# The first two raw chunks of a weight, loaded early into an idle input buffer

## The chip, the core and the metric

The kernel runs on one core of a Trainium2 chip. The core has a matrix engine (PE in the rows, with its weight loads as PEld), VectorE (DVE), ScalarE (ACT), GpSimd (POOL) and SyncE (SP, SPq for its queue of DMA issues); sixteen DMA engines move data between HBM and the on-chip memory (SBUF). The metric is device microseconds (us) of one execution, the median of the timed runs; lower is better.

## What is computed

Masked attention over 2 batches of 8 heads (768 tokens, head size 64), then two feed-forward layers on the 1536 tokens it gives (512 columns, 2048 inner columns). Cut to what matters:

```python
scores = scale * np.matmul(q, k.transpose(0, 1, 3, 2))
scores = np.where(mask, scores, -1000000000.0)     # mask: the 6-bit buckets of q and k agree
attn = softmax(scores)
x = np.matmul(attn, v)                             # per head, then (1536, 512)

h = x @ w_in                                       # first layer
g = np.where(h > 0.0, h, np.exp(np.minimum(h, 0.0)) - 1.0)
x = g @ w_out

h = x @ w_in2                                      # second layer
r = np.maximum(h, 0.0)
out = (s * (r * r) + b) @ w_out2
```

The weights arrive as 8-byte floats.

## The kernel before

**Attention** goes in units: unit u is one head of one chunk of 128 queries, 96 units in all; units 0 to 47 are batch 0 (chunks 0 to 5), 48 to 95 batch 1. A unit has its scores on PE (L358), the row maximum on DVE (L368), the exponential on ACT (L370), and then a split of the result into a high and a low 16-bit half: ACT copies the high half (L389), GpSimd subtracts (L392, tile `ph`), and SP issues a transposing DMA (L394, tile `pt`). PE then multiplies `pt` with the values (L412, tile `xacc`). The first 16 units take another way, through PE transposes (L379, L406). Three `ph` buffers rotate. After the eighth head of a chunk the result is normalised and laid into one of three input buffers `xx[0..2]` of the first layer, 512 tokens each; `xx[1]` (x_114 in an instruction's operands) is for tokens 512 to 1023, so nothing is written to it before chunk 4. `xx[2]` (x_115) serves, while it is idle, as a place for raw keys, queries and values of batch 1.

**Weights of the first layer** are streamed by the generator `w_stream`, one chunk of 512 KB per step: a step splits chunk n-3 into halves, decodes chunk n-2, and issues the load of chunk n into one of three `wraw` buffers (L167). Decoding is three DVE instructions (L194, L195, L197: an 8-byte float becomes a 4-byte one). Splitting is a copy on ACT (L188, tiles `wih`, `woh`) and a subtraction: on DVE (L204), or, for chunks that count as set aside, on GpSimd, which then also scales the chunk (L187, then L202):

```python
aside_ = n_ - 3 < aside
if aside_:
    nc.gpsimd.tensor_scalar(w, w, SW, None, op0=ALU.mult)
```

Here n_ is the step. The 16 chunks of `w_in` have 12 set aside, the 16 chunks of `w_out` none. The stream of `w_in` starts at unit 2, that of `w_out` is chained behind it once the first layer's products run.

**The first layer** (`moe1`) goes over six blocks of 256 tokens: `up` multiplies with `w_in` (L531, tile `h`), `down` with `w_out` (L531, tile `x2p`). Its products and the steps of attention are woven together by a credit count; two of three product slots also take a step of the weight stream (`w1_step`). When 40 units have been started and the stream isn't through, the rest of it is run through at once, ahead of any further unit:

```python
while live["w1"] and nxt["s"] >= (C - 1) * H:
    w1_step()
```

In what follows this stretch is called the drain. The second layer (`up2`, `down2`) runs after that, with attention over. A scheduler with a modelled clock puts the instructions of each engine in order, so that a new instruction also shifts its neighbours.

Of the kernel before, what the change touches and what calls it, by code (L numbers as in the profile page):

```python
# [10 lines left out]
I32 = mybir.dt.int32  # L11
# [50 lines left out]
SC_N = 16  # L62
PRE = 4
W_FROM = 2
LN2 = 0.6931471805599453


def model_kernel(tc, q, k, v, proj, w_in, w_out, w_in2, w_out2, s2, b2, sel, pop, eye, out):
    nc = tc.nc
# [23 lines left out]
    with ExitStack() as base:  # L93
# [50 lines left out]
        def w_raw(st):  # L144
            return pool(st, "wraw", WRAW, side="right")


        def w_tiles(p, nm):
            return [p.tile([128, KF, 512], F16, name=f"{nm}{x}") for x in "hl"]

        def w_in_chunks(dst, dram):
            w = dram.bitcast(I32)
            return [((lambda a, f=f: dst(f)) if callable(dst) else [d[:, f, :] for d in dst], w[:, 256 * f:256 * f + 256].rearrange("(k p) n -> p k n", p=128))
                    for f in range(KF)]

        def w_col_chunks(dst, dram):
            w = dram.bitcast(I32)
            return [([z[:, f:f + 4, 128 * d:128 * d + 128] for z in dst],
                     w[128 * f:128 * f + 512, 256 * d:256 * d + 256].rearrange("(k p) n -> p k n", p=128))
                    for d in range(KM) for f in range(0, KF, 4)]  # L160

        def w_load(ch, wraw):
            t = wraw.tile([128, 512, 2], I32, tag="w", name="wraw")
            o = t.rearrange("p n t -> p (n t)")
            if len(ch[1].shape) == 3:
                o = o.rearrange("p (k n) -> p k n", k=ch[1].shape[1])
            nc.sync.dma_start(out=o, in_=ch[1])  # L167
            return t

        def w_stream(chunks, wraw, words, delay=0, aside=0):  # L170
            loaded, joined = [], []
            for n_, ch in enumerate(chunks + [None] * 3):
                with late_by(delay):
                    done = joined.pop(0) if joined else None
                    if done:
                        (dst, _), w = done
                        w = w.bitcast(F32)
                        if callable(dst):
                            dst = dst(w)
                            done = dst and (None, w)  # L180
                    if done:
                        hi, lo = dst
                        if len(hi.shape) == 3:
                            w = w.rearrange("p (k n) -> p k n", k=hi.shape[1])
# [3 lines that stand above are left out]
                        nc.scalar.activation(out=hi, in_=w, func=ACTF.Copy, scale=1.0 if aside_ else SW)  # L188
                    if len(loaded) == 2 or (ch is None and loaded):
                        c0, t = loaded.pop(0)  # L190
                        a, x = words()
                        a, x = a.bitcast(I32), x.bitcast(I32)
                        low, top = t[:, :, 0], t[:, :, 1]
                        nc.vector.tensor_scalar(x, top, 3, 0x3FFFFFFF, op0=ALU.logical_shift_left, op1=ALU.bitwise_and)  # L194
                        nc.vector.scalar_tensor_tensor(out=x, in0=low, scalar=29, in1=x,  # L195
                                                       op0=ALU.logical_shift_right, op1=ALU.bitwise_or)
                        nc.vector.scalar_tensor_tensor(out=a, in0=top, scalar=-0x40000000, in1=x,  # L197
                                                       op0=ALU.bitwise_and, op1=ALU.bitwise_or)
                        joined.append((c0, a))
                    if done:  # L200
                        if aside_:
                            nc.gpsimd.tensor_tensor(out=lo, in0=w, in1=hi, op=ALU.subtract)  # L202
                        else:
                            nc.vector.scalar_tensor_tensor(out=lo, in0=w, scalar=SW, in1=hi,  # L204
                                                           op0=ALU.mult, op1=ALU.subtract)
                    if ch is not None:
                        loaded.append((ch, w_load(ch, wraw)))
                yield
# [153 lines left out]
        def u_soft(u):  # L362
# [5 lines left out]
            nc.vector.tensor_scalar(f, sps.pop(u), CLAMP, None, op0=ALU.min, op1=ALU.min, accum_out=mx)  # L368
            (nc.gpsimd if U0 <= u < MXP else nc.vector).tensor_scalar(mx, mx, sm / (SQ * SQ), 10.0 * LN2, op0=ALU.mult, op1=ALU.add)  # L369
            nc.scalar.activation(out=f, in_=f, func=ACTF.Exp, scale=-sm / (SQ * SQ), bias=mx,  # L370
# [44 lines left out]
        xx = [xs_.tile([128, 2 * KM, 512], F16, name=f"x{i}") for i in range(B * C // 4)]  # L415
# [53 lines left out]
        nxt = {"s": 0, "av": 0, "soft": [], "split": [], "lag": LAG0}  # L469
# [339 lines left out]
        if True:  # L809
# [3 lines left out]
            for hp, nm in ((0, "k"), (0, "q"), (1, "k"), (1, "q")):  # L813
# [5 lines left out]
            wdec = w_raw(wdst), lambda: (wst.tile([128, 512], F32, tag="wa", name="wa"),  # L819
                                         ring.take("w", [128, 512], F32, "wx"))  # L820
            ws1 = w_stream(w_in_chunks(wi, w_in), *wdec, aside=ASIDE)
            n = 0
            for _ in att:
                n += 1
                if nxt["s"] >= W_FROM and n % WN == 0:
                    next(ws1, None)
                if done_chunks[0] == BLOCKS1[0]:
                    break
# [12 lines left out]
                gp[0] = pool(gst1, "gp1", 1)  # L841

            wo = w_tiles(wop, "wo")
            ws1 = chain(ws1, w_stream(w_col_chunks(wo, w_out), *wdec))
            live = {"w1": True, "att": True}
            credit = 0.0

# [24 lines left out]
            for ks, cost in enumerate(moe1(wi, wo, gp, next_gp, tmp, tmpg, att_step)):  # L872
# [7 lines left out]
                if not live["att"] and ws2 is None:  # L880
# [5 lines left out]
                    wraw = w_raw(wlate)  # L886
# [12 lines left out]
                    ch = ci[:W2PRE]  # L899
# [80 lines left out]
```

## Time and profile before

| what | value |
|---|---|
| runs, median (lowest to highest) | 716.36 us (713.94 to 717.16) |
| profiled execution, its own time | 715.27 us |
| its span | 713.5 us |
| PE busy | 659.6 us, 92% |
| DVE busy | 516.6 us, 72% |
| ACT busy | 417.2 us, 58% |
| GpSimd busy | 272.7 us, 38% |
| mean granted clock of PE | 0.986 |

The own time is what the runs measure; the span is the stretch that the trace covers, 1.8 us less. Busy shares are means over stages that are unlike each other.

### The profile page before, as it was taken

Reading aid. Unit: us, or ns where it says so; the run is one execution under the profiler, and the core shown is the slowest. Engines: PE = TensorE matmul, PEld = TensorE weight load, DVE = VectorE, ACT = ScalarE, POOL = GpSimd, SP = SyncE. Lnnn points to the kernel's source line nnn. Section 1 sums busy time; section 2 is a strip of 40 time slices with the busy share of each in tenths; the row PEclk is TensorE's granted clock in tenths of the full one; section 3 lists DMA queues with packets and bytes.
Section 4 is the critical chain, followed back from the end, with each engine's and each line's share of the span. In section 5 each row is a group of like instructions: output and inputs, shape, how many; then the busy total and the mean of one; then the engine's idle time right before and its main releaser. Section 6 shows DMA issues by size and latency. Waiting matters only on the chain.

```text
span 713.5 us, 15214 instructions
## 1 busy us (share of the span) xinstructions
PE 659.6 (92%) x6192; PEld 504.0 (71%) x6192; DVE 516.6 (72%) x885; ACT 417.2 (58%) x687; POOL 272.7 (38%) x219
## 2 busy tenths in 40 slices
PE   2789869888887999999999999999999999999998
PEld 0368657676666777888888988874444446888887
DVE  5688899888878468645744699439999726999730
ACT  2897679874797887756755333234555525555520
POOL 1257778873445278945854421311211200000000
PEclk9999979999999999999999999999999999999999
DMA  9984599999899588966768545004453000000100
GB/s 234 259 222 135 159 223 225 205 229 219 178 208 215 88 142 159 154 119 123 123 112 120 132 153 175 1 25 125 121 149 115 0 1 1 16 30 32 45 30 30
DMA packets 206742, 89.73 MB, mean 126 GB/s; under 512 B 171856, under 2 KB 203344, under 8 KB 206672
## 3 DMA queue, kind: packets, MB, share of 16 engines
q1 hardware_dynamic: 206080, 88.63, 56.4%
q8 instruction: 48, 0.79, 0.5%
q10 hardware_dynamic: 592, 0.14, 0.1%
q14 instruction: 22, 0.18, 0.1%
HBM read 43.13 MB, written 3.15 MB: 65 GB/s over the span
## 4 chain that ended last, share of the span: by engine, by line
PE 59%; DMA 11%; ACT 10%; DVE 7%; issue 6%; POOL 5%; SPq 0%; DVEq 0%; ACTq 0%; POOLq 0%
PE h L531 24%; PE y L775 15%; PE x2p L531 10%; DMA pt<-ph 6%; PE s L358 4%; POOL ph L392 3%; ACT p L370 3%; PE xacc L412 3%; ACT ph L389 2%; PE xacc L406 1%; DVE e L546 1%; DMA k<-src 1%; ACT gh L551 1%; PE pT L379 1%; DVE p L368 1%
## 5 line engine op out<-in xcount | busy, mean ns | idle before, releaser
L392 POOL TENSOR_TENSOR ph<-p,ph 128x768 f16<-128x768 f32 x80 | 133.9, 1679 | 65.3 <-ACT ph L389 45.7
L531 PE MATMUL h<-x,wih 128*128 128x256 f16 x768 | 132.5, 276 | 0.1
L531 PE MATMUL h<-x,wi 128*128 128x512 f16 x576 | 124.5, 379 | 0.0
L368 DVE TENSOR_SCALAR_CACHE_REDUCE p<-s 128x768 f32<-128x768 f32 x96 | 91.0, 950 | 44.4 <-PE s L358 42.1
L370 ACT ACTIVATE p<-p,mx 128x768 f32<-128x768 f32 x96 | 89.1, 928 | 46.4 <-DVE mx L369 40.5
L775 PE MATMUL y<-wqh,a 128*128 128x256 f16 x672 | 110.3, 273 | 0.0
L775 PEld LDWEIGHTS <-a 128*128 128x128 f16 x1008 | 98.5, 98 | 11.8
L531 PE MATMUL x2p<-gh,woh 128*128 128x256 f16 x384 | 104.8, 274 | 2.0 <-ACT woh L188 1.0
L531 PE MATMUL x2p<-gh,wol 128*128 128x256 f16 x384 | 105.0, 274 | 1.5 <-DVE wol L204 1.5
L531 PE MATMUL h<-x,wil 128*128 128x256 f16 x384 | 106.0, 276 | 0.0
L531 PE MATMUL x2p<-gl,woh 128*128 128x256 f16 x384 | 104.9, 274 | 0.5 <-POOL gl L554 0.4
L531 PEld LDWEIGHTS <-wi 128*128 128x128 f16 x576 | 56.3, 98 | 67.8
L775 PE MATMUL y<-wql,a 128*128 128x256 f16 x336 | 91.2, 273 | 0.0
L358 PE MATMUL s<-k,q 128*128 128x512 f16 (+1 forms) x384 | 81.0, 336 | 4.8 <-DVE p L368 4.5
L531 PEld LDWEIGHTS <-woh 128*128 128x128 f16 x768 | 74.8, 98 | 13.5 <-ACT woh L188 1.4
L531 PEld LDWEIGHTS <-wih 128*128 128x128 f16 x768 | 75.2, 99 | 12.8 <-issue 0.5
L554 POOL TENSOR_TENSOR gl<-g,gh 128x512 f16<-128x512 f32 x48 | 58.1, 1211 | 63.3 <-ACT gh L551 62.7
L412 PE MATMUL xacc<-vv,pt 128*128 128x64 f16 x1440 | 57.7, 195 | 18.2 <-DMA pt<-ph 18.2
L412 PEld LDWEIGHTS <-pt 128*128 128x128 f16 x1440 | 53.9, 99 | 24.3 <-DMA pt<-ph 21.2
L389 ACT ACTIVATE ph<-p 128x768 f16<-128x768 f32 x80 | 66.6, 836 | 5.2 <-DMA pt<-ph 4.1
L567 DVE SCALAR_TENSOR_TENSOR g<-h,sbs,r 128x512 f32<-128x512 f32 x48 | 35.7, 745 | 23.6 <-ACT r L564 23.6
L564 ACT ACTIVATE r<-h 128x512 f32<-128x512 f32 x48 | 28.2, 590 | 39.5 <-PE h L531 39.5
(121 smaller groups left out, 1043.3 us busy)
## 6 DMA issues: line engine op xcount, KB each, us to landing
wraw<-in_moe_w_in SPq DMA_DIRECT2D x32, 512.0 KB, 3.8
wraw<-in_moe_w_out SPq DMA_DIRECT2D x32, 512.0 KB, 3.9
out<-y SPq DMA_DIRECT2D x10, 256.0 KB, 2.0
raw<-in_k SPq DMA_DIRECT2D x6, 384.0 KB, 4.4
raw<-in_q SPq DMA_DIRECT2D x6, 384.0 KB, 4.4
v<-in_v SPq DMA_DIRECT2D x4, 384.0 KB, 5.1
pt<-ph SPq DMA_TRANSPOSE x80, 4.0
x<-in_k SPq DMA_DIRECT2D x2, 384.0 KB, 5.0
```

Source lines behind the costliest of these rows:

```text
L358: nc.tensor.matmul(p[:, a0:a1], w[b, hp][:, j, c, :], kf[:, a0:a1], start=(x == 0), stop=(x == 1))
L368: nc.vector.tensor_scalar(f, sps.pop(u), CLAMP, None, op0=ALU.min, op1=ALU.min, accum_out=mx)
L370: nc.scalar.activation(out=f, in_=f, func=ACTF.Exp, scale=-sm / (SQ * SQ), bias=mx, accum_out=sums[b, c][:, h:h + 1])
L379: nc.tensor.transpose(p[:, 128 * cc:128 * cc + 128], f[:, 128 * cc:128 * cc + 128], ident)
L389: nc.scalar.activation(out=t[:, 0, :], in_=f, func=ACTF.Copy)
L392: nc.gpsimd.tensor_tensor(out=t[:, 1, :], in0=f, in1=t[:, 0, :], op=ALU.subtract)
L412: nc.tensor.matmul(acc, o[:, C * x + cc, :], vv[:, j, cc, y, :], start=(z == 0 and cc == 0), stop=(z == 2 and cc == C - 1))
L531: nc.tensor.matmul(p, ws[a](kk), xs[b](kk), start=(kk == 0 and z == 0), stop=(kk == n_kk - 1 and z == 2))
L554: nc.gpsimd.tensor_tensor(out=gl, in0=t["g"], in1=gh, op=ALU.subtract)
L564: nc.scalar.activation(out=t["r"], in_=p, func=ACTF.Relu, scale=UN)
L567: nc.vector.scalar_tensor_tensor(out=g, in0=p, scalar=sb["s"], in1=t["r"], op0=ALU.mult, op1=ALU.mult)
L775: nc.tensor.matmul(p, a[:, xa, kk, :], wq[y][:, WQ[n], kk, :], start=first and k == 0, stop=k == 3 * K2 - 1, skip_group_check=True)
```

## The change

The first two chunks of `w_out` are loaded during the first units of attention, behind the steps in which 6 and 8 units have been started, into the two halves of `xx[1]`. The stream of `w_out` begins with these two as already loaded and fetches the other 14 itself. The destination of a chunk is looked up late, since the tiles of `w_out` don't exist yet when the list of chunks is made.

```diff
+EARLY = [6, 8]
...
+        def w_early(ch, x):
+            t = xx[1].rearrange("p a t -> p (a t)").bitcast(I32)[:, 1024 * x:1024 * x + 1024]
+            nc.sync.dma_start(out=t.rearrange("p (k n) -> p k n", k=ch[1].shape[1]), in_=ch[1])
+            return ch, t.rearrange("p (n t) -> p n t", t=2)
+
-        def w_stream(chunks, wraw, words, delay=0, aside=0):
-            loaded, joined = [], []
+        def w_stream(chunks, wraw, words, delay=0, aside=0, loaded=(), late_dst=False):
+            loaded, joined = list(loaded), []
...
+                        if late_dst:
+                            dst = dst()
...
-            n = 0
+            n, early = 0, []
+            co1 = w_col_chunks(lambda: wo, w_out)
             for _ in att:
                 n += 1
+                if len(early) < len(EARLY) and nxt["s"] >= EARLY[len(early)]:
+                    early.append(w_early(co1[len(early)], len(early)))
...
-            ws1 = chain(ws1, w_stream(w_col_chunks(wo, w_out), *wdec))
+            ws1 = chain(ws1, w_stream(co1[len(early):], *wdec, loaded=early, late_dst=True))
```

Two things follow from `w_stream` as it stands. It has two steps fewer (14 chunks and 3 closing steps, not 16 and 3). And its steps count from 0 with two chunks in hand, so that the first two are split in steps 1 and 2, where n_ - 3 is below 0: they count as set aside although `aside` is 0 for this stream, and go to GpSimd.

The queue of SP in the first units, before (v_576 are the values of the last pair of heads, x_115 is `xx[2]`):

```order
L292 DMA_TRANSPOSE q_373<-src 128x12x128
L252 DMA v_455<-in_v 128x2x384
L167 DMA wraw<-in_moe_w_in 128x4x256
L252 DMA v_576<-in_v 128x2x384
L252 DMA x_115<-in_k 128x2x384
L252 DMA x_115<-in_q 128x2x384
L167 DMA wraw<-in_moe_w_in 128x4x256 x5
```

And in the changed kernel, where the line numbers are higher by up to 11 and the same values are v_577:

```order
L300 DMA_TRANSPOSE q_373<-src 128x12x128
L260 DMA v_455<-in_v 128x2x384
L168 DMA wraw<-in_moe_w_in 128x4x256
L173 DMA x_114<-in_moe_w_out 128x4x256
L260 DMA v_577<-in_v 128x2x384
L173 DMA x_114<-in_moe_w_out 128x4x256
L260 DMA x_115<-in_k 128x2x384
L260 DMA x_115<-in_q 128x2x384
L168 DMA wraw<-in_moe_w_in 128x4x256 x5
```

One of the two new loads stands ahead of the last values, one behind them.

GpSimd, at the place where the first chunks of `w_out` are split, before (`gl` is the low half of a result of `up`, `mx` a scaled row maximum):

```order
L392 TENSOR_TENSOR ph<-p,ph 128x768
L369 TENSOR_SCALAR mx<-mx 128x1
L392 TENSOR_TENSOR ph<-p,ph 128x768
L554 TENSOR_TENSOR gl<-g,gh 128x512
L369 TENSOR_SCALAR mx<-mx 128x1
L392 TENSOR_TENSOR ph<-p,ph 128x768
L369 TENSOR_SCALAR mx<-mx 128x1
L554 TENSOR_TENSOR gl<-g,gh 128x512
```

And in the changed kernel (L195 is L187 of before, L210 is L202, L400 is L392):

```order
L195 TENSOR_SCALAR wa<-wa 128x512
L400 TENSOR_TENSOR ph<-p,ph 128x768
L377 TENSOR_SCALAR mx<-mx 128x1
L400 TENSOR_TENSOR ph<-p,ph 128x768
L562 TENSOR_TENSOR gl<-g,gh 128x512
L195 TENSOR_SCALAR wa<-wa 128x512
L210 TENSOR_TENSOR wol<-wa,woh 128x4x128
L377 TENSOR_SCALAR mx<-mx 128x1
L400 TENSOR_TENSOR ph<-p,ph 128x768
L562 TENSOR_TENSOR gl<-g,gh 128x512
L377 TENSOR_SCALAR mx<-mx 128x1
L210 TENSOR_TENSOR wol<-wa,woh 128x4x128
```

Four instructions are new on GpSimd; two subtractions (L204) are gone from DVE.

ACT at the drain, before (the last rows ahead of batch 1's first split of keys, `src<-x_115`):

```order
L188 ACTIVATE woh<-wa 128x4x128
L389 ACTIVATE ph<-p 128x768
L370 ACTIVATE p,sum<-p,mx 128x768
L389 ACTIVATE ph<-p 128x768
L370 ACTIVATE p,sum<-p,mx 128x768
L389 ACTIVATE ph<-p 128x768
L188 ACTIVATE woh<-wa 128x4x128 x5
L260 ACTIVATE src<-x_115 128x12x64
```

And in the changed kernel (L196 is L188, L378 is L370, L397 is L389, L268 is L260):

```order
L196 ACTIVATE woh<-wa 128x4x128
L378 ACTIVATE p,sum<-p,mx 128x768
L397 ACTIVATE ph<-p 128x768
L378 ACTIVATE p,sum<-p,mx 128x768
L397 ACTIVATE ph<-p 128x768
L196 ACTIVATE woh<-wa 128x4x128
L378 ACTIVATE p,sum<-p,mx 128x768
L397 ACTIVATE ph<-p 128x768
L196 ACTIVATE woh<-wa 128x4x128 x3
L268 ACTIVATE src<-x_115 128x12x64
```

Three chunks, not five, are left for the unbroken run; the other two stand among the units ahead of it.

## Rows read from the trace of the kernel before

**Rows 1.** The page, part 1: busy us (share of span), instructions.

```profile
PE 659.6 (92%) x6192; PEld 504.0 (71%) x6192; DVE 516.6 (72%) x885; ACT 417.2 (58%) x687; POOL 272.7 (38%) x219
```

**Rows 2.** Stretches: length, busy of each engine, granted clock, DMA share, GB/s.

```profile
48.00:52.00 4.00, 2.81 (x13) 1.69 (x12) 2.83 (x6) 3.98 (x7) 1.38 (x1) 0.75 0.09 18
96.00:108.00 12.00, 12.00 (x122) 9.42 (x120) 11.03 (x18) 10.53 (x20) 6.85 (x8) 0.78 1.10 228
108.00:124.00 16.00, 14.87 (x193) 12.57 (x191) 15.12 (x28) 14.79 (x28) 13.87 (x13) 1.00 1.08 229
124.00:132.00 8.00, 5.87 (x68) 4.13 (x65) 7.62 (x14) 6.95 (x14) 7.51 (x9) 0.79 1.05 202
132.00:168.00 36.00, 33.52 (x417) 28.26 (x415) 29.79 (x55) 27.03 (x47) 25.55 (x25) 1.00 1.05 222
168.00:180.00 12.00, 9.47 (x116) 7.31 (x114) 10.40 (x15) 3.19 (x6) 1.64 (x1) 1.00 0.93 240
...
300.00:713.00 413.00, 408.86 (x3510) 306.95 (x3508) 281.06 (x433) 191.29 (x307) 94.17 (x63) 1.00 0.33 78
```

**Rows 3.** Waits of PE, 96 to 182 us: total us, times, longest.

```profile
PE xacc L412 <- DMA pt<-ph: 5.5, 4, 2.0
PE x2p L531 <- DVE wol L204: 1.5, 3, 0.9
PE x2p L531 <- ACT woh L188: 1.0, 2, 0.7
```

**Rows 4.** Waits of PE, 182 to 320 us, same columns.

```profile
PE pbit L320 <- DMA k<-src: 2.0, 1, 2.0
```

**Rows 5.** DMA, 96 to 171 us: queue, issues with us to landing.

```profile
q1 hardware_dynamic: 43218, 16.71, 105.9%
...
wraw<-in_moe_w_out SPq DMA_DIRECT2D x14, 512.0 KB, 4.6
pt<-ph SPq DMA_TRANSPOSE x22, 5.0
```

**Rows 6.** DMA queue, 48 to 90 us, same columns.

```profile
q1 hardware_dynamic: 7875, 5.89, 50.5%
```

**Rows 7.** SP timeline, 36 to 41 us: start us, length us, issue.

```profile
38.32 0.83 SPq L252 DMA_DIRECT2D v<-in_v  x1
```

**Rows 8.** Tile `v`, 36 to 48 us.

```profile
DMA to landing us min/median/max: 5.2/5.6/6.1
```

**Rows 9.** PE timeline, 44 to 48 us (in brackets: idle before, releaser).

```profile
45.25 1.45 PE L406 MATMUL xacc<-v,pt 128*128 128x64 f32 x12
47.44 0.77 PE L379 MATMUL pT<-ident,p 128*128 128x128 f32 x5 [0.74 <-ACT k L337]
```

**Rows 10.** GpSimd groups, 0 to 230 us: count, busy us, mean ns, idle before.

```profile
L187 POOL TENSOR_SCALAR wa<-wa 128x512 f32<-128x512 f32 x12 | 17.9, 1489 | 15.1 <-DVE wa L197 9.3 <-DVE mx L369 5.3
...
L202 POOL TENSOR_TENSOR wil<-wa,wih 128x512 f16<-128x512 f32 x12 | 14.8, 1240 | 2.5 <-ACT wih L188 2.0
```

**Rows 11.** Waits of SP's queue, 84 to 185 us.

```profile
SPq L394 <- POOL ph L392: 14.7, 8, 2.9
```

**Rows 12.** GpSimd timeline, at 120 and at 168 us.

```profile
120.68 1.65 POOL L392 TENSOR_TENSOR ph<-p,ph 128x768 f16<-128x768 f32 x1 [1.47 <-ACT ph L389]
...
168.28 1.64 POOL L392 TENSOR_TENSOR ph<-p,ph 128x768 f16<-128x768 f32 x1 [1.71 <-ACT ph L389]
```

**Rows 13.** DVE group of the subtraction, 96 to 182 us.

```profile
L204 DVE SCALAR_TENSOR_TENSOR wol<-wa,woh 128x512 f16<-128x512 f32 x16 | 13.6, 848 | 2.8 <-ACT woh L188 2.8
```

**Rows 14.** DVE timeline at 168 us.

```profile
168.70 1.77 DVE L204 SCALAR_TENSOR_TENSOR wol<-wa,woh 128x512 f16<-128x512 f32 x1 [2.05 <-ACT woh L188]
```

**Rows 15.** ACT timeline, the drain.

```profile
168.05 0.61 ACT L188 ACTIVATE woh<-wa 128x512 f16<-128x512 f32 x1
171.10 0.63 ACT L188 ACTIVATE woh<-wa 128x512 f16<-128x512 f32 x1 [2.44 <-DVE wa L197]
...
179.25 0.63 ACT L188 ACTIVATE woh<-wa 128x512 f16<-128x512 f32 x1 [2.08 <-DVE wa L197]
```

More of the change, by code (lines that the diff above doesn't have):

```diff
@@ L157, in w_col_chunks @@
             w = dram.bitcast(I32)
-            return [([z[:, f:f + 4, 128 * d:128 * d + 128] for z in dst],
+            return [((lambda d=d, f=f: [z[:, f:f + 4, 128 * d:128 * d + 128] for z in dst()]),
                      w[128 * f:128 * f + 512, 256 * d:256 * d + 256].rearrange("(k p) n -> p k n", p=128))
```

## The prediction

> **What bounds the kernel now.** I read the page first. PE is busy 92% of the span [rows 1], so time can only come from the 8% in which it isn't, or from work on it that ran at the lower clock. Busy time by stretches says where that is. Behind 300 us PE is busy 408.86 of 413 us: nothing is to be had there. The change touches the stretch from 38 to about 181 us, and the part of it in which attention, the weight stream and the first layer run side by side is 96 to 180 us. There PE is busy 12.00, 14.87, 5.87, 33.52 and 9.47 us of 84, so it idles 8.3 us, and twice the granted clock falls below 1, a mean of its full level (2.4 GHz) and its half (1.2): 0.78 over 12 us and 0.79 over 8 us, which is (0.22 x 12) + (0.21 x 8) = 4.3 us of PE time at the full clock [rows 2]. The other engines are as full: from 108 to 124 us DVE is busy 15.12, ACT 14.79, GpSimd 13.87 of 16 us, and the DMA engines are at 1.05 to 1.10 from 96 to 168 us [rows 2]. So no single engine bounds this stage; the waits of PE must say which one comes last.
>
> They do. Between 96 and 182 us PE waits 5.5 us, four times, for the transposing DMA of a unit (`pt`), and 2.5 us for the halves of `w_out` (1.5 for DVE's, 1.0 for ACT's) [rows 3]. The second kind lies in the drain: ACT casts the last chunks with a decoding on DVE between each two, at 171.10 to 179.25 us, three intervals of 2.72 us [rows 15]. Behind it PE waits another 2.0 us for the first keys of batch 1 [rows 4], whose split stands behind the drain on ACT.
>
> **The change, part by part.**
>
> *Two loads more at 38 to 41 us.* The last values are issued at 38.32 us [rows 7] and land 5.2 to 6.1 us later [rows 8], at 43.5 to 44.4. PE reads them at 45.25 at the earliest, so 0.8 to 1.7 us are to spare, and it waits 0.74 us for ACT a little later anyway [rows 9]. One new load of 512 KB goes ahead of them, the other behind. What a load takes of the DMA engines: from 48 to 90 us, where loads are nearly all there is, 5.89 MB took 50.5% of 42 us [rows 6], 21.2 us or 3.6 us per MB; so 1.9 us for 512 KB. The values land up to 1.9 us later; of that 0.8 to 1.7 are covered and 0.74 more can be taken out of the wait that follows. Between 0 and 1.1 us; I take +0.3, near the low end, since the cover nearly matches the delay. SP took 0.83 us to issue a load there [rows 7], and behind the new ones stand only loads. Those of `w_in` can slip too, but the DMA engines stand at 0.09 from 48 to 52 us [rows 2], so the backlog is gone by then. Cost nothing beyond the 0.3; without that gap it would be another 1.9 us.
>
> *Two loads fewer from 96 us on.* The stage has 14 loads of `w_out` and 22 transposes in the 75 us up to 171 us, and its queue is at 105.9% [rows 5]. Two loads at 3.6 us per MB are 3.8 us of it. If the DMA engines alone set the pace, the stage gets 3.8 us shorter; if DVE or GpSimd does, nothing comes of it. PE's waits for transposes there are 5.5 us [rows 3], so there is room for the whole. But these are four single waits, and SP's own transposes waited 14.7 us for GpSimd's subtraction in this stage [rows 11], so the transposes are late from both ends. I take -1.6, somewhat under the middle of 0 and -3.8.
>
> *GpSimd.* Two scalings at 1.49 us and two subtractions at 1.24 us are new [rows 10]: +5.5 us, all at the place where GpSimd is busy 13.87 of 16 us [rows 2]. The units' subtractions queue behind them, then SP's transposes, then PE. The next gap of GpSimd there is 1.47 us at 120 us [rows 12], so up to 4.0 us are left, and 5.5 if that gap moves away. At the other end nothing, if PE has first-layer products to do meanwhile. I take +2.0, half of 4.0: PE's waits for transposes (5.5 us in all) show that it can't hide all of it.
>
> *DVE.* Two subtractions of 0.85 us go [rows 13]: -1.7 us of DVE time. DVE is busy 63.6 of the 72 us up to 168 us [rows 2], and the decoding that leaves the drain comes into this stretch (next), so I count no gain for it: it pays for that.
>
> A rule that speaks against this trade: the subtraction at 168.70 us took 1.77 us [rows 14], 0.92 more than the mean of 0.85 [rows 13], while a GpSimd subtraction ran from 168.28 to 169.92 us [rows 12]. The Trainium skill (SBUF — State Buffer, section Who interferes with whom) says that a DVE instruction with two SBUF inputs contends with a GpSimd instruction that reads SBUF, and that the later one is held for the whole of the other. The trace agrees. By this rule each of the four new instructions can hold up one such instruction of DVE; at 0.92 us each that would be 3.7 us more, and the sum below would be +1.4 us instead of -2.3.
>
> *The drain.* ACT's unbroken run has three casts instead of five. At 2.72 us each [rows 15] it is 5.4 us shorter; the two chunks are done among the units ahead of it. What PE can win is what it waits: 2.5 us in the drain [rows 3] and 2.0 us behind it [rows 4], 4.5 in all. At the other end nothing: if the units ahead come later by what was put among them (two chunks of 2.72 us on DVE, less the 1.7 it is rid of, is 3.7 us, against 8.4 us that DVE idles up to 168 us), the last chunks come no earlier. I take -3.0, two thirds of 4.5, since DVE has the idle time but not where it is wanted.
>
> *Sum.* +0.3 - 1.6 + 2.0 - 3.0 = -2.3 us. The profiled execution has 715.27 us of its own, 713.5 of them span; it would be 713.0. The median of the runs shown is 716.36, 1.1 above it; I carry that over: **714.1 us**.
>
> **Rivals.**
>
> *Faster: the drain pays in full and GpSimd's work is hidden.* PE's waits of 4.5 us go, the loads bring 1.6, the front costs 0.3: -5.8 us, 710.6. With the loads at their bound of 3.8 it is -8.0, 708.4. For it: PE had 33.52 of 36 us of work between 132 and 168 us [rows 2], most of it products that can be done while a transpose is late. Against it: the stretch from 108 to 132 us, where GpSimd is fullest, is where PE idles most.
>
> *Slower: GpSimd becomes the bound.* Its 5.5 us reach PE, and by the hold-ups of DVE (0.92 us each) another 3.7. With the drain at -3.0 and the front at +0.3, and nothing from the loads, this is +6.5 us: 722.9; with GpSimd's gap of 1.47 us used, 721.4. It decides from the point where more than 6.3 us of these 9.2 reach PE (6.3 - 3.0 + 0.3 = 3.6, the 0.5%). For it: three `ph` buffers rotate through ACT, GpSimd, SP and a DMA of 5.0 us [rows 5], so that a late unit delays the third one behind it; the longest of PE's waits for a transpose is 2.0 us [rows 3], and from 124 to 132 us, where PE is busy 5.87 of 8 us, the granted clock falls to 0.79 [rows 2], so a wait can cost more than itself. The rule of the skill named above is a part of it. Against it: two thirds must hit, and fewer loads shorten the same rotation.
>
> *The change doesn't do what it says.* The decoding on DVE, not the loading, sets when a chunk is ready (in the drain ACT waits for DVE and never for a load [rows 15]), so the loads were hidden already and only the order changes: 716.4.
>
> **How the numbers follow.** About 0.5%, 3.6 us, is what a measurement can tell here: the three runs lie 3.2 us apart. Chances: the forecast 0.42 (of it 0.05 past the bound on the fast side and 0.02 on the slow side), the faster rival 0.30, the slower one 0.16, no effect 0.12. Faster by over 0.5%: 0.05 + 0.30 = 0.35. Slower: 0.16 + 0.02 = 0.18. Within: 0.35 + 0.12 = 0.47. The range for 8 in 10 reaches from 709.0, just above the faster rival's bound, to 719.8, which leaves out the upper two thirds of the slower one. The likeliest case's own range is 711.5 to 717.
>
> **What would show it.** Right: no wait of PE for `woh` or `wol` behind unit 40, the wait for the first keys below 1 us, ACT's last three casts 2.7 us apart and the first split of batch 1's keys several us ahead of 181 us; landing times of `pt` under 5.0 us. GpSimd's term shows in PE's waits for `pt` between 105 and 130 us: above 4 us the term is bigger than I took it, and below 2 it is hidden. The front shows in a wait of PE for the last values at 45 us. Wrong would be the prediction above all if PE's waits for transposes grow by more than the 4.5 us that the drain can give back, or if the new order shifts waits into batch 1, behind 181 us, which no term here counts.

## The result, and the profile after

The change makes the kernel slower: 718.79 us in the median of 11 runs (716.74 to 723.46) against 713.79 of 11 runs of the kernel before (711.26 to 718.11). The ratio, worked out from all these runs, is 1.0077, with a 95% interval of 1.0055 to 1.0098; the two medians alone would give 1.0070. (The three runs shown ahead, median 716.36, lay in the upper part of that spread; I had carried their 1.1 us over into the forecast.)

The profiled execution took 718.79 us of its own, with a span of 717.0, which is 3.5 us more than before. Busy times on the page of the changed kernel, as in [rows 1]:

```profile
PE 660.8 (92%) x6192; PEld 504.4 (70%) x6192; DVE 519.8 (72%) x883; ACT 419.6 (59%) x687; POOL 276.6 (39%) x223
```

GpSimd has its four instructions more, DVE two fewer but 3.2 us more of busy time, and PE works 1.2 us more and idles 2.3 more. Where, the same stretches as in [rows 2] and one more say (length, then busy us of PE, PEld, DVE, ACT and GpSimd, granted clock, DMA share, GB/s):

```profile
96.00:108.00 12.00, 12.00 (x120) 9.44 (x118) 11.43 (x18) 10.53 (x20) 7.12 (x7) 0.81 1.11 207
108.00:124.00 16.00, 14.32 (x180) 11.96 (x179) 13.56 (x26) 14.54 (x28) 15.18 (x15) 1.00 0.69 157
124.00:132.00 8.00, 6.98 (x87) 5.77 (x84) 8.00 (x12) 5.64 (x11) 7.33 (x7) 1.00 0.83 193
132.00:168.00 36.00, 31.29 (x348) 24.14 (x346) 33.51 (x55) 26.16 (x46) 25.10 (x25) 0.91 1.10 222
168.00:180.00 12.00, 11.55 (x168) 9.91 (x166) 11.31 (x19) 6.25 (x11) 5.25 (x5) 1.00 1.08 212
180.00:200.00 20.00, 15.24 (x164) 11.49 (x162) 15.70 (x32) 15.45 (x31) 8.87 (x9) 0.91 0.99 205
```

Up to 132 us PE is not behind. Its loss comes later. From 132 to 168 us it idles 4.7 us (before 2.5) at a mean granted clock of 0.91, which is 0.09 x 36 = 3.2 us of PE time at the full clock (before none). From 180 to 200 us it idles 4.8 and loses 1.8 to the clock (before 3.2 and none). In the drain between them it idles 0.4 (before 2.5). Idle time and clock together, 132 to 200 us: 15.0 us against 8.2. The row of before that [rows 2] doesn't have:

```profile
180.00:200.00 20.00, 16.77 (x193) 13.31 (x192) 17.59 (x33) 16.55 (x32) 8.66 (x9) 1.00 0.87 165
```

The first difference lies earlier, from 108 to 132 us: GpSimd is full (15.18 of 16 us), and the share of the DMA engines falls from 1.08 to 0.69 in the first 16 of them, so the transposes and loads aren't queueing for the DMA engines there; they are issued late. The share by itself doesn't tell what the kernel loses: of the runs below, it is 0.92 with no chunk set aside, where a part of the fall is the two loads that are gone, and 0.68 with `gl` on DVE, and neither loses time.

GpSimd of the changed kernel in that stretch (start us, length us, instruction):

```profile
108.29 1.49 POOL L195 TENSOR_SCALAR wa<-wa 128x512 f32<-128x512 f32 x1
109.86 1.69 POOL L400 TENSOR_TENSOR ph<-p,ph 128x768 f16<-128x768 f32 x1
...
114.75 1.49 POOL L195 TENSOR_SCALAR wa<-wa 128x512 f32<-128x512 f32 x1
116.32 1.16 POOL L210 TENSOR_TENSOR wol<-wa,woh 128x512 f16<-128x512 f32 x1
...
121.28 1.16 POOL L210 TENSOR_TENSOR wol<-wa,woh 128x512 f16<-128x512 f32 x1
```

DVE of the changed kernel, same columns (in brackets idle time before it and its releaser): the decodings of the first four chunks (L205), two subtractions (L212), and the row maxima (L376) of units 24 and 32, to which the experiments come back:

```profile
106.61 0.68 DVE L205 SCALAR_TENSOR_TENSOR wa<-x,wx 128x512 int32<-128x512 int32 x1
107.21 0.95 DVE L376 TENSOR_SCALAR_CACHE_REDUCE p<-s 128x768 f32<-128x768 f32 x1
...
110.00 0.69 DVE L205 SCALAR_TENSOR_TENSOR wa<-x,wx 128x512 int32<-128x512 int32 x1
...
117.51 0.69 DVE L205 SCALAR_TENSOR_TENSOR wa<-wraw,wx 128x512 int32<-128x512 int32 x1 [1.07 <-POOL wol L210]
...
120.17 0.98 DVE L212 SCALAR_TENSOR_TENSOR wol<-wa,woh 128x512 f16<-128x512 f32 x1
121.19 0.69 DVE L205 SCALAR_TENSOR_TENSOR wa<-wraw,wx 128x512 int32<-128x512 int32 x1
...
123.72 2.00 DVE L212 SCALAR_TENSOR_TENSOR wol<-wa,woh 128x512 f16<-128x512 f32 x1
...
142.76 0.95 DVE L376 TENSOR_SCALAR_CACHE_REDUCE p<-s 128x768 f32<-128x768 f32 x1
```

And before, the first and third decoding and the maxima of the same two units:

```profile
107.11 0.68 DVE L197 SCALAR_TENSOR_TENSOR wa<-wraw,wx 128x512 int32<-128x512 int32 x1
107.71 0.95 DVE L368 TENSOR_SCALAR_CACHE_REDUCE p<-s 128x768 f32<-128x768 f32 x1
...
116.24 0.67 DVE L197 SCALAR_TENSOR_TENSOR wa<-wraw,wx 128x512 int32<-128x512 int32 x1
...
137.52 0.95 DVE L368 TENSOR_SCALAR_CACHE_REDUCE p<-s 128x768 f32<-128x768 f32 x1
```

There are two `wa` buffers. The first chunk holds one from 106.61 until GpSimd has subtracted from it, at 116.32 + 1.16 = 117.48 us, and 0.03 us later DVE, idle for 1.07 us, writes the third chunk into it. Before, the third was decoded 9.1 us behind the first; now it is 10.9 us behind. The second chunk holds the other from 110.00 to 121.28 + 1.16 = 122.44, and the fourth is decoded when DVE has subtracted from the third (120.17 + 0.98 = 121.15).

What waits for that is SP's queue, 106 to 134 us (waiting for: total us, times, longest):

```profile
SPq L168 <- DVE wa L205: 6.2, 3, 3.2
SPq L402 <- POOL mx L377: 5.7, 2, 4.6
SPq L402 <- POOL gl L562: 5.6, 3, 2.1
SPq L402 <- POOL ph L400: 2.8, 1, 2.8
```

And before:

```profile
SPq L167 <- DVE wa L197: 1.3, 1, 1.3
```

Before, the loads (L167 there) waited 1.3 us for a decoding; now 6.2, and the transposes behind them in the same queue with them. From 106 to 133 us SP issues five transposes of `pt` where it issued seven. This wait isn't what sets the time, though: in runs below that lose next to nothing it is 5.0 us (`gl` on DVE), 6.8 (idle work at the first chunks) and 4.9 (the words of both chunks in `xx[1]`).

PE waits of the changed kernel, 96 to 182 us and then 182 to 320, to be set beside [rows 3] and [rows 4]:

```profile
PE xacc L420 <- DMA pt<-ph: 5.2, 4, 2.0
PE xacc L420 <- DVE wx L203: 1.7, 1, 1.7
PE x2p L539 <- ACT gh L559: 0.5, 1, 0.5
...
PE xacc L420 <- DMA pt<-ph: 8.7, 8, 2.0
PE pbit L328 <- DMA k<-src: 1.8, 1, 1.8
```

The waits for `woh` and `wol` are gone, as forecast; the wait for the first keys is not (2.0, now 1.8), and behind 182 us 8.7 us are waited for transposes, where it was 5.9.

### The profile page after: what moved, and what is told of

Its sections match the earlier page's. It is cut to its first block, busy times and chain, and to the rows that moved or that the text cites. A ratio compares the mean times of both kernels' runs of the same rounds, so it can differ in the third digit from the quotient of the medians.

```text
span 717.0 us, 15222 instructions
## 1 busy us (share of the span) xinstructions
PE 660.8 (92%) x6192; PEld 504.4 (70%) x6192; DVE 519.8 (72%) x883; ACT 419.6 (59%) x687; POOL 276.6 (39%) x223
## 4 chain that ended last, share of the span: by engine, by line
PE 57%; DMA 7%; DVE 6%; issue 4%; ACT 4%; POOL 3%; SPq 0%; DVEq 0%; POOLq 0%; ACTq 0%
PE h L539 26%; PE y L783 15%; PE x2p L539 10%; DMA pt<-ph 5%; PE s L366 4%; PE xacc L420 3%; POOL ph L400 2%; DVE e L554 1%; DVE p L376 1%; ACT p L378 1%; DMA k<-src 1%; ACT gh L559 1%; DVE g L556 1%; ACT ph L397 1%; POOL gl L562 1%
## 5 line engine op out<-in xcount | busy, mean ns | idle before, releaser
L400 POOL TENSOR_TENSOR ph<-p,ph 128x768 f16<-128x768 f32 x80 | 132.5, 1659 | 81.0 <-ACT ph L397 56.0
L378 ACT ACTIVATE p<-p,mx 128x768 f32<-128x768 f32 x96 | 89.1, 929 | 49.9 <-DVE mx L377 40.8
L376 DVE TENSOR_SCALAR_CACHE_REDUCE p<-s 128x768 f32<-128x768 f32 x96 | 91.1, 952 | 37.5 <-PE s L366 35.8
L366 PE MATMUL s<-k,q 128*128 128x512 f16 (+1 forms) x384 | 82.6, 342 | 6.0 <-DVE p L376 4.0
L397 ACT ACTIVATE ph<-p 128x768 f16<-128x768 f32 x80 | 66.9, 838 | 9.7 <-DMA pt<-ph 8.4
```

The costliest lines, as they stand in the source:

```text
L366: nc.tensor.matmul(p[:, a0:a1], w[b, hp][:, j, c, :], kf[:, a0:a1], start=(x == 0), stop=(x == 1))
L397: nc.scalar.activation(out=t[:, 0, :], in_=f, func=ACTF.Copy)
L400: nc.gpsimd.tensor_tensor(out=t[:, 1, :], in0=f, in1=t[:, 0, :], op=ALU.subtract)
```

## The experiments

Each kernel was timed in five rounds beside the kernel before; ratios are to that, with 95% intervals. "Set aside" means that GpSimd scales and subtracts a chunk.

**The parts one by one.** The change without anything set aside:

```diff
-... *wdec, loaded=early, late_dst=True))
+... *wdec, loaded=early, late_dst=True, aside=-3))
```

> The changed kernel with the two early chunks split on DVE as all the others (aside = -3 for the stream of w_out), so GpSimd gets none of the four new instructions. If GpSimd's 5.5 us are what made the change slower: within 2 us of before or faster by up to 4 (ratio 0.994 to 1.003). If a rearranged order is what costs, wherever it comes from: slower by 3 to 6 us again (1.004 to 1.009), since the order of PE differs from before here too. If the two early loads themselves cost: slower by about 5 us (1.007).

Measured 0.9995 [0.9971, 1.002]: the whole loss is gone, and no gain comes out. The opposite, the kernel before with two chunks set aside and no early load:

```diff
-ws1 = chain(ws1, w_stream(w_col_chunks(wo, w_out), *wdec))
+ws1 = chain(ws1, w_stream(w_col_chunks(wo, w_out), *wdec, aside=2))
```

> The kernel before, with nothing loaded early, but the first two chunks of w_out split on GpSimd (aside = 2). DVE, ACT and GpSimd then stand in nearly the order of the changed kernel. If GpSimd's work or the order that it brings is the cause: slower by 4 to 7 us (1.005 to 1.010), since the gain of the shorter drain is missing too. If the loads are the cause: within 1 us of before (0.998 to 1.002).

1.0054 [1.0031, 1.0077], 3.9 us. The early loads alone, never read (the kernel before; its orders of PE, DVE and GpSimd are unchanged, ACT has one split of values two places later):

```diff
+                if len(early) < 2 and nxt["s"] >= [6, 8][len(early)]:
...
+                    nc.sync.dma_start(out=t_..., in_=w_out.bitcast(I32)[...])
```

> The kernel before, with the two early loads issued into the idle buffer behind units 6 and 8 and never read; the stream of w_out loads all 16 chunks itself. All engines but SP keep the order of before. If the loads cost at the front: slower by 0.3 to 1.1 us by my sum (1.000 to 1.002), by 5 us (1.007) if they are the whole cause. If GpSimd or the order is the cause: no difference that can be measured.

0.9988 [0.9967, 1.001]. One early chunk instead of two, none set aside (`EARLY = [6]`, `aside=-3`):

> One chunk early (behind unit 6) and none on GpSimd. PE, ACT and GpSimd keep the order of before, DVE and SP all but. If the order is what costs: no difference (0.998 to 1.002). If one load fewer in the full stage of DMA brings what I counted: faster by 0.8 us (0.999), by 1.9 at the bound (0.997). If an early load at the front is the cause: slower by 2 to 3 us (1.003).

0.9989 [0.9969, 1.0009]. And two, none set aside, loaded later, behind 12 and 14 units (`EARLY = [12, 14]`, `aside=-3`):

> The change without GpSimd's part (aside = -3) and with the two early loads behind units 12 and 14, where the DMA engines are half idle. If the loads and the shorter drain bring nothing, wherever they stand: as e1 (0.997 to 1.002). If e1 lost at the front what it won later: faster by 1 to 3 us (0.996 to 0.999).

1.0012 [0.9994, 1.0031]. So the loads cost nothing and give nothing that can be measured, wherever they stand; the two set-aside chunks make the loss.

**The dose.** One chunk set aside and then four, in the changed kernel (`aside=-1` and `aside=2`; in this stream steps 1 and 2 have n_ - 3 below 0):

> The changed kernel with one chunk of w_out split on GpSimd instead of two (aside = -1), so half of the dose: 2.7 us on GpSimd. If GpSimd's queue ahead of the transposes is the cause and its work adds up: half of the loss, about 2 us slower than before (1.002 to 1.004). If any rearranged order can cost or not by chance: anywhere between 0.997 and 1.008.

> The changed kernel with four chunks of w_out split on GpSimd instead of two (aside = 2), 10.9 us on GpSimd. If the work on GpSimd adds up: 8 us slower than before (1.008 to 1.013). If only what stands at one crowded place counts: as with two (1.005 to 1.008). By chance of the order: between 0.997 and 1.008.

1.0039 [1.0018, 1.006] and 1.0103 [1.0076, 1.013]. With 0, 1, 2 and 4 chunks the loss is none, 0.4, 0.8 and 1.0%. Two chunks set aside in the drain (numbers 13 and 14), in the kernel before:

```diff
-aside_ = n_ - 3 < aside
+aside_ = n_ - 3 < aside or n_ - 3 in late
```

> The kernel before with two chunks split on GpSimd as well, but chunks 13 and 14 of w_out, which fall into the drain, where GpSimd was busy 1.6 of 12 us. The same four instructions, at a place where no transpose is queued behind them. If what counts is that the units' subtractions queue behind them: no loss (0.997 to 1.002). If it is GpSimd work in itself, as the longer way of a chunk, or DVE held up by it: slower as with the first two chunks (1.003 to 1.008).

1.0028 [1.0009, 1.0046], between the two forecasts: it costs there too, about half of what it costs among the units. Fewer of `w_in` set aside, in the kernel before:

```diff
-ASIDE = 12
+ASIDE = 10
```

> The kernel before with 10 instead of 12 chunks of w_in split on GpSimd (ASIDE = 10): 5.5 us less on GpSimd ahead of 96 us, where it is busy 11.2 of 12 us from 84 to 96 us and PE waits 6.7 us for the first transposes, and two subtractions more on DVE, which is busy 10.8 of 12 us there. If GpSimd's queue is what the transposes wait for there as well: faster by 2 to 5 us (0.993 to 0.997). If DVE is as much of a bound there: no difference, or slower by the 2 us of the subtractions (1.000 to 1.003).

1.0027 [1.0005, 1.0048], a miss: taking work from GpSimd is no gain as such.

**Relief for GpSimd.** The first four `gl` of block 0 on DVE, in the changed kernel, and as a control in the kernel before:

```diff
-nc.gpsimd.tensor_tensor(out=gl, in0=t["g"], in1=gh, op=ALU.subtract)
+eng.tensor_tensor(out=gl, in0=t["g"], in1=gh, op=ALU.subtract)
...
+nc.vector if i == 0 and f0 < 8 else nc.gpsimd
```

> The changed kernel with the first four low halves of the first layer (gl) subtracted on DVE instead of GpSimd: 4.6 us less on GpSimd at the place where the two chunks went to it, and four instructions of 0.7 us more on DVE. The two chunks stay on GpSimd. If the queue of GpSimd ahead of the transposes is the cause, relief of another kind must help as much: from 1.008 down to 1.000 to 1.003. If the chunks' own longer way (scaling and subtraction on GpSimd hold the buffers that DVE decodes into) is the cause: 1.006 to 1.010, as with the change or worse, since DVE gets more.

> The same move of four gl onto DVE in the kernel before, where the place was full but not past its capacity. If GpSimd bounded the stage there as well: faster by 2 to 4 us (0.994 to 0.997). If GpSimd, DVE and the DMA engines are balanced before the change: no difference or up to 2 us slower (0.999 to 1.003).

1.0003 [0.9984, 1.0022]: with the two chunks still set aside the loss is gone. The control got slower, 1.0049 [1.002, 1.0077], a miss: four subtractions more on DVE cost when GpSimd isn't too full. The scaled maxima on DVE (`MXP = 16` in place of 44), in both kernels:

> The changed kernel with the small scaling of the row maximum (mx) on DVE for all units (MXP = 16): 28 instructions of 0.2 to 0.5 us less on GpSimd, and ACT's exponential no longer waits behind GpSimd's queue. By GpSimd's queue as the cause: from 1.008 down to 1.002 to 1.005, as only a part of the relief lies at the crowded place. By the chunks' own longer way: no relief, 1.006 to 1.010.

> The same move of mx onto DVE in the kernel before. If GpSimd bounded the stage: faster by 2 to 4 us (0.994 to 0.997). If the engines are balanced: within 2 us (0.997 to 1.003).

1.0064 [1.004, 1.0088] and 1.0031 [1.001, 1.0053]; the first is a miss of the theory of GpSimd's queue, which wanted 1.002 to 1.005, and the second lies just outside the range of either forecast.

**Work without a chunk.** Four scalings on GpSimd that nobody reads, behind the splits of the first two chunks, and behind those of chunks 13 and 14, in the kernel before (`idle=(13, 14)`):

```diff
+if n_ - 3 in idle:
...
+    for _ in range(2):
+        nc.gpsimd.tensor_scalar(z, hi, SW, None, op0=ALU.mult)
...
+... *wdec, idle=(0, 1)))
```

> The kernel before with four instructions more on GpSimd, each scaling a high half of the first two chunks of w_out into the idle input buffer, which nobody reads: 1.2 to 1.5 us each, at the same place as the four of the change. The chunks themselves are split on DVE as before. By the queue ahead of the units' subtractions: slower by 3 to 6 us (1.004 to 1.009), as with e2. By the chunks' longer way or the buffers that they hold: within 1.5 us of before (0.998 to 1.002).

> The same four idle instructions behind chunks 13 and 14, in the drain, where GpSimd is nearly idle. By the queue: no loss (0.998 to 1.002). If the 0.3% of e9 come from the rearranged order around batch 1's start: 1.001 to 1.004 again. If they come from the chunks' longer way in the drain: no loss here.

1.0018 [0.9992, 1.0044] and 0.9996 [0.998, 1.0012]. The first upset the theory that I had by then, though its interval still reaches the 1.004 that the queue wanted. The second says that in the drain GpSimd's time costs nothing: the 1.0028 of the two chunks set aside there comes from the chunks' longer way (PE waits 2.4 us for GpSimd's `wol` there, and not at all in the run with idle work) or from the order. And idle work at the first chunks does delay the units. Their row maxima, units 24 and 32, in that run (DVE, start us, length us):

```profile
106.33 0.95 DVE L372 TENSOR_SCALAR_CACHE_REDUCE p<-s 128x768 f32<-128x768 f32 x1
...
143.85 0.94 DVE L372 TENSOR_SCALAR_CACHE_REDUCE p<-s 128x768 f32<-128x768 f32 x1
```

That is 37.5 us for eight units. In the changed kernel, by its rows on DVE above, it is 142.76 - 107.21 = 35.5. Before, it was 137.52 - 107.71 = 29.8. So units that come late don't make the kernel slow by themselves. The other half of a set-aside chunk is its `wa` buffer.

**The buffers.** The last three runs take chunks out of the two `wa` buffers, so that their decoded words go to `xx[1]`; the first two of them leave all the work on GpSimd. The changed kernel with the second chunk's words there (the first half is free by then; it can't take the first chunk's, whose raw words lie in it), the kernel before with both set aside and in `xx[1]`, and the kernel before with both in `xx[1]` and nothing set aside:

```diff
-a, x = words()
+a, x = words(True) if len(joined_n) in own else words()
...
+def own_wa():
+    return xx[1].rearrange("p a t -> p (a t)").bitcast(F32)[:, 0:512]
...
-lambda: (wst.tile([128, 512], F32, tag="wa", name="wa"),
+lambda o=False: (own_wa() if o else wst.tile([128, 512], F32, tag="wa", name="wa"),
```

> The changed kernel, with the 4-byte words of the second early chunk decoded into the first half of xx[1], which is idle by then, so that only one of the two set-aside chunks occupies one of the two wa buffers. In the changed kernel DVE waits 1.1 us for GpSimd to free a wa buffer between 106 and 134 us, and SP's loads wait 6.2 us for decodings there (before: 1.3), with transposes queued behind them. Theory of GpSimd's queue (the added instructions stand ahead of the units' subtractions): the loss stays, 1.005 to 1.010 of the time before. Theory of the held buffers (the longer way of a set-aside chunk holds wa, so decodings, loads and the transposes behind them in SP's queue come late): most of it goes, 0.998 to 1.004.

> The kernel before with the first two chunks of w_out set aside, as in the run of that alone (1.0054), and the words of both in xx[1], outside of the wa buffers. Theory of GpSimd's queue: 1.004 to 1.007, as there. Theory of the held buffers: 0.998 to 1.002.

> The kernel before with the words of the first two chunks of w_out in xx[1] and nothing set aside: PE, GpSimd and SP keep the order of the kernel before. The control of the two other runs: 0.998 to 1.002 by the theory of GpSimd's queue; by that of the held buffers the same, or faster down to 0.995, since DVE has two more buffers for two chunks.

1.0017 [0.9995, 1.004], 1.0013 [0.999, 1.0036] and, for the control, 1.0001 [0.9977, 1.0024]. The theory of GpSimd's queue is refuted as the whole cause: it wanted 1.004 to 1.010 for the first two. The second of them, set beside its twin with `wa` buffers (1.0054), on GpSimd:

```profile
107.31 1.49 POOL L187 TENSOR_SCALAR x<-x 128x512 f32<-128x512 f32 x1
108.88 1.69 POOL L393 TENSOR_TENSOR ph<-p,ph 128x768 f16<-128x768 f32 x1
...
113.77 1.49 POOL L187 TENSOR_SCALAR x<-x 128x512 f32<-128x512 f32 x1
115.34 1.16 POOL L203 TENSOR_TENSOR wol<-x,woh 128x512 f16<-128x512 f32 x1
```

The same instructions at the same distances as in the changed kernel. Its decodings of the first three chunks and the eighth on DVE:

```profile
105.63 0.68 DVE L198 SCALAR_TENSOR_TENSOR x<-wraw,wx 128x512 int32<-128x512 int32 x1
109.02 0.69 DVE L198 SCALAR_TENSOR_TENSOR x<-wraw,wx 128x512 int32<-128x512 int32 x1
...
112.55 0.68 DVE L198 SCALAR_TENSOR_TENSOR wa<-wraw,wx 128x512 int32<-128x512 int32 x1
...
135.00 0.69 DVE L198 SCALAR_TENSOR_TENSOR wa<-wraw,wx 128x512 int32<-128x512 int32 x1
```

The third chunk follows 6.9 us behind the first (changed kernel 10.9), the eighth 29.4 us behind (37.0). Its eight units still take 37.4 us. Its stretches from 132 to 168 and 180 to 200 us, columns as above:

```profile
132.00:168.00 36.00, 30.84 (x365) 25.07 (x364) 31.49 (x56) 26.57 (x47) 27.20 (x25) 0.95 0.98 202
...
180.00:200.00 20.00, 17.75 (x215) 14.12 (x213) 15.77 (x31) 16.49 (x31) 9.65 (x9) 1.00 1.11 210
```

From 180 to 200 us PE is busy 17.75 us at full clock, where the changed kernel had 15.24 at 0.91.

## Why the prediction was wrong

Two things decide the stage: when attention's units come, and when the chunks of `w_out` come, since PE can fill a late unit with products only if the weights are there. The table has both from DVE's timelines: the time from the row maximum of unit 24 to that of unit 32, and from the decoding of the first chunk to that of the eighth. The fourth column is PE's idle time plus the part lost to the clock, 132 to 200 us, from the stretches. The fifth is the time from the maximum of unit 24 to that of unit 95, the last. All four are from one profiled execution each; the ratio is from all runs.

| kernel | units 24 to 32, us | chunks 1 to 8, us | PE loses, us | units 24 to 95, us | ratio |
|---|---|---|---|---|---|
| before | 29.8 | 37.6 | 8.2 | 280.4 | 1 |
| no chunk set aside | 27.0 | 34.3 | 10.2 | 279.9 | 0.9995 |
| `gl` on DVE, changed kernel | 30.6 | 35.8 | 9.4 | 279.8 | 1.0003 |
| idle work at the first chunks | 37.5 | 29.0 | 10.6 | 281.0 | 1.0018 |
| words in `xx[1]`, both set aside | 37.4 | 29.4 | 10.2 | 282.5 | 1.0013 |
| words in `xx[1]`, changed kernel | 35.2 | 27.5 | 11.1 | 282.2 | 1.0017 |
| one set aside | 32.4 | 34.5 | 9.8 | 284.2 | 1.0039 |
| **changed kernel** | 35.5 | 37.0 | 15.0 | 284.3 | 1.0077 |
| set aside alone | 35.5 | 37.0 | 15.5 | 285.2 | 1.0054 |
| four set aside | 39.2 | 39.2 | 16.4 | 288.5 | 1.0103 |

Where the units are 5 to 8 us late and the chunks 8 to 10 us early, little is lost. Where the units are late and the chunks no earlier (the last three rows), PE loses 15.0 to 16.4 us from 132 to 200 us, and 8.2 to 11.1 in the other rows. That stretch doesn't hold all of it: with the words of both chunks in `xx[1]` PE loses 6.6 us from 108 to 132 us, where it was 4.9 before and 2.7 in the changed kernel, and with one chunk set aside it loses 12.1 us from 200 to 300 us (before 9.5). The fifth column goes better with the ratios: 3.8 to 8.1 us over the kernel before in the last four rows, 1.8 and 2.1 with words in `xx[1]`, 0.6 with idle work.

The set-aside chunks do both: their instructions on GpSimd delay the units, and their hold on `wa` keeps DVE from using that time for the next chunks. That the set-aside chunks make the whole loss is shown, by the runs without them, with them alone, and with one and four. That the hold on `wa` makes most of it is what the runs with the words in `xx[1]` say, but they don't prove it by themselves: the mean of DVE's subtractions, 1276 to 1495 ns in the last three rows, fell to 929 and 988 ns in these two as well. Against the subtractions as the cause stand the runs with idle work (1090 ns) and with no chunk set aside (1117), which lose next to nothing. That GpSimd's fill is needed too is suggested by the `gl` on DVE, where the third chunk is as late as in the changed kernel (11.5 us behind the first) and yet nothing is lost; the same move costs 0.5% in the kernel before, so it isn't a clean relief. That the sum of the two columns is what counts is a reading made after the runs. It holds for the control with `gl` on DVE in the kernel before as well (31.2 and 41.1 us, 1.0049; units 24 to 95 take 284.5 us). It doesn't explain the 0.4% of one chunk, nor the 0.3% of two chunks in the drain and of `ASIDE = 10`, and 1.0064 with the maxima on DVE is more than its 32.0 and 37.3 us would give. Most of these runs also move the order of the instructions, and runs that only move a little work between engines cost 0.3 to 0.5%; that part stays open.

By the steps of the prediction, of which two failed by about the same amount, the gain from the loads and the drain and the cost on GpSimd:

**The front, +0.3.** Right in being near nothing: the loads alone measured 0.9988 [0.9967, 1.001]. The reason given for it was a misreading. In the changed kernel the last values are issued later and land 6.6 us after that, at 45.8 us (before 44.4), so behind the start of the group at 45.19 us, the 45.25 of [rows 9]:

```profile
39.24 0.51 SPq L260 DMA_DIRECT2D v<-in_v  x1
...
45.19 1.45 PE L414 MATMUL xacc<-v,pt 128*128 128x64 f32 x12
...
57.15 1.45 PE L414 MATMUL xacc<-v,pt 128*128 128x64 f32 x12
```

That group is the fourth, unit 3, and reads the values of another pair of heads. The last pair belongs to units 6 and 7, and PE comes to unit 6 at 57.15 us (57.47 before). So PE had 13 us to spare before, not 0.8 to 1.7, and the term should have been nothing.

**Two loads fewer, -1.6.** Not found. The changed kernel's DMA queue and transposes, 96 to 171 us, as in [rows 5]:

```profile
q1 hardware_dynamic: 39528, 14.99, 97.5%
...
pt<-ph SPq DMA_TRANSPOSE x21, 4.8
```

The queue fell from 105.9 to 97.5% and a transpose took 4.8 us, not 5.0, but the change without set-aside chunks gained nothing. The issues were late, not the DMA engines: in the changed kernel SP waits 15.2 us for `mx` and 11.8 for `ph` of GpSimd from 84 to 185 us, and 14.0 for decodings (before: 10.6, 14.7 and 8.7).

The rival "the change doesn't do what it says" had this right: the loads were hidden already. What I forecast without GpSimd's term, +0.3 - 1.6 - 3.0 = -4.3 us, can be set beside the run with no chunk set aside, which measured -0.4 us (-2.1 to +1.4). That is one half of the miss, 3.9 us, and lies in this term and in the drain's.

**GpSimd, +2.0: the other step that failed.** What the set-aside chunks cost is 3.9 us (alone, on the kernel before) to 5.9 (the changed kernel's 1.0077 less 0.9995, of 714 us), up to 3.9 us more than I took: the other half. I counted their 5.5 us on GpSimd and the queue behind them, and put them at half of 4.0. I didn't count that a set-aside chunk holds one of two `wa` buffers, for 10.9 and 12.4 us. The sign that I named also misled: PE's waits for `pt` between 105 and 130 us are 0.9 us, which I had said would mean "hidden". The price was paid 30 to 70 us later. The slower rival, "GpSimd becomes the bound" at 721.4 to 722.9 or 5.0 to 6.5 us more than before, had the engine and the size (5.0 between the medians, 5.5 by the ratio), with a chance of 0.16. The size was in part luck: it rested on GpSimd's time alone and a hold-up of DVE, 7.7 to 9.2 us, plus 0.3 at the front and less 3.0 from a drain that gave nothing. The range, up to 719.8, ended below the 720.0 at which this rival begins by its own condition, and so left out the whole of it, not two thirds.

**DVE, nothing counted.** The subtractions on DVE got longer: 14 of them took 18.2 us, a mean of 1297 ns against 848 [rows 13], which is 4.6 us more than the 16 of before took. In the row at 123.72 us above one took 2.00 us, with GpSimd's `ph` beside it from 123.53 to 125.17. This agrees with what the Trainium skill (SBUF — State Buffer, section Who interferes with whom) says and the prediction weighed: a DVE instruction with two SBUF inputs contends with a GpSimd instruction that reads SBUF. But the four new instructions are not where most of it happens, since such rows of 1.75 to 2.07 us stand at 140.76, 152.51, 161.78 and 170.94 us too, and with no chunk set aside the mean is 1117 ns (16 of them, 17.9 us) and the time unchanged. So hold-ups of this size need not cost anything; whether the further ones of the changed kernel are a part of the loss, no run here separates.

**The drain, -3.0.** It failed too: the shorter run came as forecast, and no time with it. The waits for `woh` and `wol` are gone, and ACT's last casts are 2.7 us apart, three of them (compare [rows 15]):

```profile
174.05 0.63 ACT L196 ACTIVATE woh<-wa 128x512 f16<-128x512 f32 x1 [0.94 <-DVE wa L205]
176.79 0.63 ACT L196 ACTIVATE woh<-wa 128x512 f16<-128x512 f32 x1 [2.12 <-DVE wa L205]
179.51 0.63 ACT L196 ACTIVATE woh<-wa 128x512 f16<-128x512 f32 x1 [2.09 <-DVE wa L205]
180.05 1.65 ACT L268 ACTIVATE src<-x 128x768 f16<-128x768 f32 x3
```

But the last cast ends at 180.14 us, against 179.88 before, and batch 1's split starts at 180.05, not "several us ahead of 181". The drain is shorter because the last units ahead of it come later. The row maxima of units 40 and 41, in the changed kernel and before:

```profile
168.62 0.96 DVE L376 TENSOR_SCALAR_CACHE_REDUCE p<-s 128x768 f32<-128x768 f32 x1
180.99 0.96 DVE L376 TENSOR_SCALAR_CACHE_REDUCE p<-s 128x768 f32<-128x768 f32 x1
...
162.68 0.95 DVE L368 TENSOR_SCALAR_CACHE_REDUCE p<-s 128x768 f32<-128x768 f32 x1
180.73 0.96 DVE L368 TENSOR_SCALAR_CACHE_REDUCE p<-s 128x768 f32<-128x768 f32 x1
```

Between them lie 12.4 us, before 18.05, and 12.2 with two chunks set aside and no early load at all. What the early chunks give by themselves (no chunk set aside: 14.8 us, 3.2 less) is given back: unit 48 is 3.3 us ahead of before there, unit 71 only 0.8. Nothing in this stage gained by being early.

The prediction's last sentence named a part of what came: new waits behind 181 us (8.7 us for transposes, 5.9 before), which no term counted.

## What to carry to other kernels

Work that is moved to an engine with idle time also moves the buffers it reads: count how long each holds one, not only the engine's busy time, and look at who waits for that buffer and what it could do meanwhile. A helper that numbers its steps should be read at its first steps again when it starts with work in hand: here two chunks changed engine because a count went below zero, and that side effect, not the edit's purpose, set the time. And a wait that vanishes may have vanished because something ahead of it came later; compare the end of the stage, not the wait.

## What the runs showed that I had not expected

Units delayed by 7.6 to 7.7 us in the middle of the kernel, by four idle instructions of GpSimd or by set-aside chunks with buffers of their own, cost 0.13 to 0.18% with intervals that include no change, while three quarters of that delay (5.7 us) together with held buffers cost 0.5 to 0.8%. The granted clock is a part of it: the changed kernel has 0.91 over 36 us from 132 and 0.91 again over 20 us from 180, 5.0 us of PE time in all, which no row of waits shows. It is near its lower level (1.2 GHz; 0.51 to 0.54) from 145 to 148.5, from 158.5 to 162 and from 189 to 192.5 us, and in the 4 us ahead of each PE was busy only 1.56, 1.80 and 1.24 us. Before, PE was busy 2.03 us from 184 to 188, and the clock stayed at its full level (2.4 GHz) from 132 to 200 us.
